# A planner's transfer model gets a fixed gap per transfer, and its searched order becomes a table

## The chip, the core and the metric

The kernel runs as one program on one core of a Trainium2 chip. Five engines work side by side, each with its own queue of instructions that it takes in order: PE (TensorE, matmuls and transposes; its weight loads are listed apart as PEld), DVE (VectorE), ACT (ScalarE), POOL (GpSimd) and SP (SyncE, which here only issues DMA transfers). The time is that of one execution on the device in microseconds (us); lower is better.

## The reference

Attention with rotary embedding for 4 batches of 8 heads, 576 positions, head size 64, then two matmul blocks on 2304 tokens:

```python
q_rot, k_rot = rotate(q), rotate(k)
scores = scale * q_rot @ k_rot.T              # 576 x 576 per head, softmax over rows
x = softmax(scores) @ v                       # -> 2304 x 512
h1 = ((x @ w1) * (x @ w2)) @ w3 @ w_out       # 512 -> 1024 -> 1024 -> 512
h2 = max(h1 @ u1, h1 @ u2, h1 @ u3)           # 512 -> 768
out = h2 @ u_out                              # 768 -> 512
```

The weights of the two matmul blocks arrive as 8-byte floats and are turned into 4-byte ones on the chip.

## The kernel before

**Stages.** For each of 16 pairs of heads the kernel loads q and k (`prepare`), rotates them, splits each into a high and a low part (matmuls run as three products of such parts), computes scores on PE into a two-buffer PSUM ring, takes the row maximum on DVE (L668), the exponential on ACT (L671), transposes the probabilities on PE (L676), copies them out of PSUM as a high part (L441, on ACT or DVE) and a low part (L708, DVE), and multiplies by v (`pv`). Beside this, in the first 200 us, weights are converted (`convert`): a 512 KB load into `raw` (two buffers), an ACT pass (L506), a DVE shift (L509) and a DVE merge (L511). From the converted w3 and w_out, `fold` makes the product w3 @ w_out: 8 blocks of 4 PE tasks (tile `m`), each block copied to `ga` and written to memory (`wp_d`). `gates` multiplies attention's output by w1 and w2 (tile `m` too). After attention come the rest of the fold (`fold_rest`), the product with it (`y_unit`), the second block by a Strassen-like scheme (`u_group`, tiles `q`, `tmp`, `top`) and the last matmul.

**What sets the order.** No engine's order is written out by hand. Every piece of work is a task with an engine, a modelled duration, dependences and a priority; there are 4349 tasks, numbered in the order in which the code adds them, and 1024 of them may go on either of two engines (`k.opts`, the first one is the default). `Plan.order` is a list scheduler: it keeps a clock per engine and always emits, on the engine that is free first, the ready task of lowest priority number. The emitted order is the program order of each engine, and dependences become semaphore waits. Before the change, the priorities came from formulas in the code, moved by some 400 random moves replayed from stored seeds (`MOVES`, `move`, `draws`), which also picked the engines.

**The model of a transfer.** A load or store is an SP task of 0.5 us with a `tail`, its size in units of about 350 KB (a 512 KB `raw` load has 1.46, a 256 KB store 0.73, a 576 KB q or k load 1.64, a 160 KB store 0.5). In `order`, one clock `dma` stands for all transfers: a transfer starts when the one before is through, and not before 0.65 us after the issue; it occupies 0.95 times its tail (1.9 times before 5 us), and lands 0.3 times its tail plus 0.9 us after that.

Of the kernel before, what the change touches and what calls it, by code (L numbers as in the profile page):

```python
# [45 lines left out]
MOVES = (  # L46
# [50 lines left out]
def draws(seed):  # L97
    mask = (1 << 64) - 1
    s = (seed * 0xD1342543DE82EF95 + 1) & mask
    while True:  # L100
        s = (s + 0x9E3779B97F4A7C15) & mask
        z = ((s ^ (s >> 30)) * 0xBF58476D1CE4E5B9) & mask
        z = ((z ^ (z >> 27)) * 0x94D049BB133111EB) & mask
        yield z ^ (z >> 31)


def move(prio, pick, opts, place, seed):


    d = draws(seed)  # L110

    def uni():
        return (next(d) >> 11) * (1.0 / 9007199254740992.0)

    def stretch(parts):
        width = len(prio) / parts
        lo = uni() * (len(prio) + width) - width
        return lo, lo + width

    kind = next(d) >> 62  # L120
    if kind == 1:
        parts, share = (32, 128, 512, 2048)[next(d) >> 62], (0.03, 0.1, 0.3, 1.0)[next(d) >> 62]
        lo, hi = stretch(parts)
        for i in range(len(prio)):
            if opts[i] > 1 and lo <= place[i] < hi and uni() < share:
                pick[i] = int(uni() * opts[i])
        return
    if kind == 0:
        by, width = (0.3, 1.0, 3.0, 10.0)[next(d) >> 62], 1 << (next(d) >> 61)
        lo = int(uni() * (len(prio) + width)) - width  # L130
        x = uni() + uni() + uni() + uni() - 2.0
        for i in range(max(lo, 0), min(lo + width, len(prio))):
            prio[i] = prio[i] + by * 1.7 * x
        return
    by, share = (0.1, 0.3, 0.6, 1.5)[next(d) >> 62], (0.01, 0.03, 0.1, 0.3)[next(d) >> 62]
    parts = (1, 8, 32, 128)[next(d) >> 62]
    lo, hi = stretch(parts)
    if parts == 1:
        share *= 0.3
    for i in range(len(prio)):  # L140
        if lo <= place[i] < hi and uni() < share:
            x = uni() + uni() + uni() + uni() - 2.0
            prio[i] = prio[i] + by * 1.7 * x
# [1067 lines left out]
```

## Time and profile before

| | |
|---|---|
| median of 3 runs | 925.85 us (925.26 to 926.72) |
| profiled execution, its own time | 927.38 us |
| its span, first to last instruction | 925.4 us |
| PE busy in the span | 891.0 us (96%) |
| DVE busy | 633.0 us (68%) |
| ACT busy | 475.9 us (51%) |
| POOL busy | 342.4 us (37%) |
| DMA queue of SP | 109.29 MB, 37.4% of 16 engines' span |

The profiled execution took 1.53 us more than the median, and 1.98 us of its time lie outside the span. Busy times of PE include the time in which matmuls overlap in its pipeline. The granted clock of TensorE is given as a share of full speed (2.4 GHz); its other level is 1.2 GHz.

### The profile page before, as it was taken

Reading aid. Unit: us, or ns where it says so; the run is one execution under the profiler, and the core shown is the slowest. Engines: PE = TensorE matmul, PEld = TensorE weight load, DVE = VectorE, ACT = ScalarE, POOL = GpSimd, SP = SyncE. Lnnn points to the kernel's source line nnn. Section 1 sums busy time; section 2 is a strip of 40 time slices with the busy share of each in tenths; the row PEclk is TensorE's granted clock in tenths of the full one; section 3 lists DMA queues with packets and bytes.
Section 4 is the critical chain, followed back from the end, with each engine's and each line's share of the span. In section 5 each row is a group of like instructions: output and inputs, shape, how many; then the busy total and the mean of one; then the engine's idle time right before and its main releaser. Section 6 shows DMA issues by size and latency. Waiting matters only on the chain.

```text
span 925.4 us, 16273 instructions
## 1 busy us (share of the span) xinstructions
PE 891.0 (96%) x5922; PEld 823.8 (89%) x5922; DVE 633.0 (68%) x1133; ACT 475.9 (51%) x1054; POOL 342.4 (37%) x332
## 2 busy tenths in 40 slices
PE   1898999999999999999999999999999999999998
PEld 1666769989999999999998999999999999999886
DVE  6997988898867677687766333657988577578300
ACT  4677887876757577567544222434323322334411
POOL 3645767766436366522110000433332333232000
PEclk9999999999999999999999999999999999999999
DMA  8454546542333123310147543323324114255511
GB/s 265 134 188 153 165 154 209 149 142 84 100 103 97 44 92 93 97 50 18 37 153 213 199 127 89 103 86 97 98 86 140 55 46 148 68 163 195 201 57 68
DMA packets 80287, 110.31 MB, mean 119 GB/s; under 512 B 27984, under 2 KB 61008, under 8 KB 80208
## 3 DMA queue, kind: packets, MB, share of 16 engines
q1 hardware_dynamic: 80208, 109.29, 37.4%
q8 instruction: 46, 0.75, 0.3%
q14 instruction: 33, 0.27, 0.1%
HBM read 83.76 MB, written 25.50 MB: 118 GB/s over the span
## 4 chain that ended last, share of the span: by engine, by line
PE 80%; DVE 9%; DMA 7%; issue 2%; ACT 1%; SPq 1%; POOL 0%; DVEq 0%; ACTq 0%
PE q L423 46%; PE m L423 15%; PE t L676 7%; PE pv L423 6%; PE s L423 6%; DVE pt L708 3%; DMA raw<-in_w3t_dram 3%; DVE sm L668 2%; DMA raw<-in_w_dram 2%; DVE raw L509 1%; DMA rawc<-in_w3t_dram 1%; SPq L444 1%; DMA vr<-in_vv_dram 1%; DVE cw L511 1%; ACT pt L441 0%
## 5 line engine op out<-in xcount | busy, mean ns | idle before, releaser
L708 DVE TENSOR_TENSOR pt<-t,pt 128x320 fp32r<-128x320 f32 (+3 forms) x256 | 132.4, 528 | 34.5 <-ACT pt L441 29.4
L441 ACT CAST pt<-t 128x320 fp32r<-128x320 f32 (+3 forms) x234 | 103.5, 456 | 51.9 <-PE t L676 24.9
L423 PE MATMUL pv<-pt,v 128*128 128x256 f32 (+1 forms) x576 | 113.2, 317 | 5.1 <-DVE pt L708 4.0
L668 DVE TENSOR_REDUCE sm<-s 128x1 f32<-128x576 f32 x144 | 103.9, 749 | 19.8 <-PE s L423 18.8
L423 PE MATMUL q<-gt,wp 128*128 128x384 f32 x576 | 100.0, 334 | 0.0
L423 PEld LDWEIGHTS q<-gt,wp 128*128 128x128 f32 x576 | 99.8, 188 | 0.0
L423 PEld LDWEIGHTS pv<-pt,v 128*128 128x128 f32 x576 | 82.8, 189 | 15.7 <-DVE pt L708 9.5
L423 PE MATMUL s<-st 64*128 64x288 f32 x768 | 71.7, 316 | 18.7 <-ACT st L618 11.7
L423 PEld LDWEIGHTS s<-st 64*128 64x128 f32 x768 | 55.6, 190 | 32.5 <-ACT st L618 11.7
L423 PE MATMUL q<-yc__7620,u 128*128 128x384 f32 x378 | 71.2, 340 | 0.0
L423 PE MATMUL q<-yc__7946,u 128*128 128x384 f32 x378 | 70.8, 340 | 0.0
L423 PE MATMUL q<-yc__7376,u 128*128 128x384 f32 x378 | 70.5, 340 | 0.0
L423 PEld LDWEIGHTS q<-yc__7946,u 128*128 128x128 f32 x378 | 67.1, 188 | 0.1
L423 PEld LDWEIGHTS q<-yc__7620,u 128*128 128x128 f32 x378 | 67.1, 188 | 0.0
L423 PEld LDWEIGHTS q<-yc__7376,u 128*128 128x128 f32 x378 | 67.1, 188 | 0.0
L441 ACT COPY tmp<-q 128x384 f32<-128x384 f32 x45 | 21.5, 479 | 84.7 <-PE q L423 84.5
L441 ACT COPY ga<-q 128x512 f32<-128x512 f32 (+2 forms) x34 | 16.9, 497 | 65.6 <-PE q L423 61.6
L1066 POOL TENSOR_TENSOR tmp<-tmp 128x384 f32<-128x384 f32 x20 | 22.6, 1132 | 72.3 <-ACT tmp L441 72.3
L423 PE MATMUL q<-tail,tail 128*128 128x512 f32 x216 | 49.1, 389 | 0.0
L423 PEld LDWEIGHTS q<-tail,tail 128*128 128x128 f32 x216 | 40.5, 188 | 8.4
L522 DVE TENSOR_TENSOR gt<-gt 128x768 fp32r<-128x768 f32 x24 | 26.7, 1117 | 25.3 <-ACT gt L521 25.3
L1079 DVE TENSOR_TENSOR tmp<-q,tmp 128x384 f32<-128x384 f32 x54 | 29.9, 554 | 15.4 <-PE q L423 15.2
(1222 smaller groups left out, 2050.9 us busy)
## 6 DMA issues: line engine op xcount, KB each, us to landing
gt<-g_d SPq DMA_DIRECT2D x24, 384.0 KB
raw<-in_m_dram SPq DMA_DIRECT2D x72, 128.0 KB
raw<-in_w_dram SPq DMA_DIRECT2D x16, 512.0 KB
h_d<-top SPq DMA_DIRECT2D x36, 192.0 KB
tail<-h_d SPq DMA_DIRECT2D x36, 192.0 KB
raw<-in_wo_dram SPq DMA_DIRECT2D x12, 512.0 KB
raw<-in_w3t_dram SPq DMA_DIRECT2D x12, 512.0 KB
g_d<-ga SPq DMA_DIRECT2D x32, 160.0 KB
```

The source lines that it names most:

```text
L423: pe.matmul(o, a, b, start=start, stop=stop, **kw)
L441: (e.copy if e is act else e.tensor_copy)(o, i)
L444: return add("SP", .5, lambda: sync.dma_start(o(), src()), r, w, part, deps, prio, tail=us)
L509: add("DVE", 0.42, lambda: dve.tensor_scalar(low_word(), low_word(), 29, None, ALU.logical_shift_right), part=[raw], deps=raw.writers, pri ...
L511: add("DVE", 0.69, lambda: dve.scalar_tensor_tensor(u(), u(), 3, low_word(), ALU.logical_shift_left, ALU.bitwise_or), r=[raw], deps=[first ...
L522: either(sb(n, "DVE"), lambda on: on.tensor_tensor(sel()[:, LO], f32(sel()[:, LO]), f32(sel()[:, HI]), ALU.subtract), r=[dst], part=[dst], ...
L668: add("DVE", c_dve(S), lambda s=s, col=col: dve.tensor_reduce(sm.t[:, 0, col:col + 1], s.t[:, :, :288], axis=AX.XY, op=ALU.max, negate=Tru ...
L676: pe.transpose(o, x, ident.t)
L708: add("DVE", c_dve(n), lambda: dve.tensor_tensor(low(pt.t), src(t.t), f32(hi(pt.t)), ALU.subtract), r=[t], part=[pt], deps=[h], prio=prio)
L1066: either(sb(TN), lambda on: on.tensor_tensor(s5.t, s1.t, s5.t, ALU.add), r=[s1], w=[s5], prio=prio)
L1079: add("DVE", c_dve(TN), lambda: dve.tensor_tensor(e.t, at_(o), e.t, ALU.add), r=[accs[o]], w=[e], prio=prio)
```

## The change

A transfer that starts after 12 us now occupies the DMA clock for 0.4 us more than its bytes, and lands 0.7 us after that, whatever its size. The formulas' priorities and the stored moves are no longer used: the rank of each task stands in a table `PLACE` (a permutation of 0 to 4348, entry n for task n), and `OTHER` lists the 168 tasks that go on their second engine. What the kernel computes, its tasks, their dependences, tiles and buffers stay as they are.

```diff
-MOVES = (
-    10000024, 10000032, 10000048, 10000067, 10000110, 10000112, 10000169, 10000173, 10000183, 10000227, 10000237,
...
+PLACE = (
+    2, 0, 1, 6, 3, 7, 21, 23, 25, 27, 29, 4, 5, 10, 14, 19, 20, 22, 28, 32, 35, 38, 18, 8, 12, 9, 11, 24, 26, 36, 45,
...
-def draws(seed):
...
-def move(prio, pick, opts, place, seed):
...
+OTHER = (
+    20, 21, 48, 57, 64, 143, 149, 152, 153, 184, 273, 282, 284, 344, 364, 411, 413, 414, 415, 523, 524, 529, 552,
...
             if k.tail:
                 dma = max(dma, end + 0.65)
-                dma += (1.9 if dma < 5.0 else 0.95) * k.tail
-                end = dma + 0.3 * k.tail + 0.9
+                if dma < 12.0:
+                    dma += (1.9 if dma < 5.0 else 0.95) * k.tail
+                    end = dma + 0.3 * k.tail + 0.9
+                else:
+                    dma += 0.4 + 0.95 * k.tail
+                    end = dma + 0.7
...
-        prio = [k.prio for k in self.tasks]
-        place = {k.num: i for i, k in enumerate(self.order(prio)[1])}
-        pick = [0] * len(prio)
-        for seed in MOVES:
-            move(prio, pick, [len(k.opts) for k in self.tasks], place, seed)
+        other = set(OTHER)
         for k in self.tasks:
-            k.eng, k.dur, k.lock = k.opts[pick[k.num]]
-        best = self.order(prio)
+            k.eng, k.dur, k.lock = k.opts[k.num in other]
+        best = self.order(PLACE)
```

**The tables read against the order before.** Sorted by `PLACE`, a task stands on average 6 places of 4349 from where it was emitted before, at most 94. The first 24 tasks on PE, the first 10 on ACT and the first 4 on SP are the same. The moves in the first 100 us that the next sections speak of, by number of the task on its engine:

| task | engine | number before | number in the table |
|---|---|---|---|
| second exponential of pair 0 (33) / v of pair 1 (158) | ACT | 11 / 10 | 10 / 11 |
| shift L509 and merge L511 of the first w_out chunk (2107, 2108) | DVE | 22, 38 | 14, 17 |
| load of the third w_out chunk (2113) | SP | 28 | 21 |
| its shift and merge (2115, 2116) | DVE | 51, 56 | 24, 40 |
| the four PE tasks of `fold(0)` (2125 to 2128) | PE | 46, 48, 50, 53 | 30, 34, 39, 45 |
| load of w3 chunk f=5 (2171), the one issued at 67.22 us | SP | 48 | 40 |
| load of w3 chunk f=3 (2151) | SP | 42 | 37 |

The engine differs for 83 tasks: 37 go from ACT to DVE, 28 from POOL to DVE, 12 from DVE to POOL, 4 from DVE to ACT, and one each way between ACT and POOL. By their starts in the trace before, none lies ahead of 28 us; 7 lie between 50 and 200 us (6 of them onto DVE, one from POOL to ACT); 13 between 350 and 400 us, all onto DVE; 26 between 650 and 725 us (19 onto DVE, 7 from it).

## Rows read from the trace of the kernel before

**Rows 1.** Busy time by stage: start:end, length, each engine's busy us (instructions), clock, DMA.
```profile
0.00:28.00 28.00, 8.94 (x45) 7.29 (x47) 18.21 (x23) 13.19 (x26) 12.14 (x13) 1.00 0.72 224
28.00:150.00 122.00, 111.75 (x733) 83.09 (x732) 107.11 (x197) 97.55 (x233) 74.38 (x62) 0.99 0.53 166
150.00:475.00 325.00, 323.63 (x2640) 304.00 (x2639) 247.92 (x477) 216.24 (x539) 158.66 (x145) 1.00 0.29 89
475.00:925.00 450.00, 446.72 (x2512) 429.44 (x2510) 259.75 (x439) 148.91 (x260) 97.18 (x114) 1.00 0.38 122
```
**Rows 2.** PE's waits from 28 to 150 us: sum us, times, longest.
```profile
PE pv L423 <- DVE pt L708: 3.8, 6, 1.5
PE t L676 <- DVE pt L708: 1.4, 4, 0.9
PE t L676 <- DVE sm L683: 1.2, 2, 0.9
...
PE s L423 <- ACT p__474 L671: 1.2, 1, 1.2
```
**Rows 3.** DVE's waits on transfers, 25 to 150 us.
```profile
DVE raw L509 <- DMA raw<-in_w3t_dram: 3.2, 3, 1.4
DVE raw L509 <- DMA raw<-in_w_dram: 2.1, 2, 1.2
```
**Rows 4.** Timeline of PE, 36 to 80 us: start, us, instruction [idle before].
```profile
46.24 1.06 PE L423 MATMUL s<-st,z__109 128*128 128x288 f32 x6 [1.22 <-ACT p__474 L671]
...
67.32 0.28 PE L676 MATMUL t<-ident,sm 128*9 128x128 f32 x1 [0.92 <-DVE sm L683]
...
76.10 0.41 PE L423 MATMUL pv<-pt,v 128*128 128x320 f32 x1 [1.54 <-DVE pt L708]
77.42 0.33 PE L676 MATMUL t<-ident,p__528 128*128 128x128 f32 x1 [0.90 <-DVE pt L708]
```
**Rows 5.** The chain of waits between 60 and 80 us: start, us, what.
```profile
67.22 6.05 DMA raw<-in_w3t_dram
...
73.29 1.58 DVE raw L509
```
**Rows 6.** Timeline of SP: issues from 58 to 68 us.
```profile
59.76 0.99 SPq L444 DMA_DIRECT2D raw<-in_w3t_dram  x2
60.80 0.42 SPq L444 DMA_DIRECT2D wp_d<-ga  x1
63.17 0.33 SPq L444 DMA_DIRECT2D qk__688<-in_qk_dram  x1
...
66.50 0.33 SPq L444 DMA_DIRECT2D wp_d<-ga  x1
```
**Rows 7.** Timeline of ACT: the exponential at 19.39, two loads issued in a row.
```profile
18.75 0.72 ACT L638 CAST v<-vr 128x640 fp32r<-128x640 f32 x1 [0.20 <-DMA vr<-in_vv_dram]
19.39 0.73 ACT L671 ACTIVATE p__187<-s,sm 128x576 f32<-128x576 f32 x1
...
73.28 0.68 ACT L506 ACTIVATE w<-raw 128x512 f32<-128x512 f32 x1 [1.90 <-DMA raw<-in_w3t_dram]
...
74.48 0.68 ACT L506 ACTIVATE w<-raw 128x512 f32<-128x512 f32 x1 [0.21 <-DMA raw<-in_w3t_dram]
```
**Rows 8.** Timeline of DVE, 13 to 35 us.
```profile
21.88 0.76 DVE L668 TENSOR_REDUCE sm<-s 128x1 f32<-128x576 f32 x1 [1.54 <-PE s L423]
...
26.73 1.64 DVE L509 TENSOR_SCALAR raw<-raw 128x512 uint32<-128x512 uint32 x1
28.29 0.68 DVE L708 TENSOR_TENSOR pt<-t,pt 128x512 fp32r<-128x512 f32 x1
...
32.16 0.69 DVE L441 CAST pt<-t 128x512 fp32r<-128x512 f32 x1
```
**Rows 9.** Busy time by stage, as in rows 1, around DVE's fullest stretches.
```profile
50.00:200.00 150.00, 143.55 (x1005) 114.99 (x1005) 129.90 (x231) 120.60 (x287) 100.36 (x84) 1.00 0.55 171
...
640.00:800.00 160.00, 160.00 (x909) 160.00 (x908) 121.21 (x229) 48.29 (x93) 53.80 (x77) 1.00 0.28 89
```

More of the change, by code (lines that the diff above doesn't have):

```diff
@@ L42 @@
 TERMS = ((HI, HI), (LO, HI), (HI, LO))
-MOVES = (
[47 rows of a table removed]
-)
-def draws(seed):
[L98 to L104, printed above, removed]
-def move(prio, pick, opts, place, seed):
[L110 to L143, printed above, removed]
+PLACE = (
[221 rows of a table added]
+)
+OTHER = (
[9 rows of a table added]
+)
 class Task:
```

274 rows, old and new, of tables (MOVES, OTHER, PLACE) are left out of this document.

## Prediction

> **What bounds the kernel now.** I read four views, from coarse to fine. First the busy time by stage [rows 1], columns PE, PEld, DVE, ACT, POOL: from 150 us on PE is never out of work for long. It is idle for 325 - 323.63 = 1.4 us up to 475 us, and for 3.3 us after that, which is its last matmul's end, the copy out and the last store. So three quarters of the run are PE-bound, and no order of tasks shortens them, since the change takes no matmul away. What an order can win lies ahead of 150 us: 28 - 8.9 = 19 us of idle PE before 28 us and 122 - 111.75 = 10.25 us between 28 and 150 us. There DVE is busy for 107.1 of 122 us, 88%, the most loaded engine beside PE.
>
> Second, who PE waits for between 28 and 150 us [rows 2]: the low part of the probabilities on DVE (3.8 + 1.4 us), the softmax sums on DVE (1.2), the exponentials on ACT (1.2 for one of them), which wait in turn for DVE's maxima. PE waits for no transfer itself. Third, what DVE waits for [rows 3]: 3.2 + 2.1 = 5.3 us in front of L509, the first DVE step of a weight conversion, for a load of 512 KB that has not landed. DVE takes its queue in order, so everything behind L509 stands too, the softmax among it. Fourth, the chain of waits from 60 to 80 us shows one such case whole [rows 5]: a load issued at 67.22 lands at 73.27, L509 runs until 74.87, and PE meanwhile has its two idle stretches of 1.54 and 0.90 us [rows 4].
>
> **The transfer model against the trace.** This load is the one that the old formula misses. From the issues ahead of it [rows 6] (a second q/k load like that of 63.17 follows it), by hand: the pair at 59.76 starts at 59.76 + 0.5 + 0.65 = 60.91; old occupancies are 1.39 for a raw load, 0.69 for a wp_d store, 1.56 for a q or k load. The queue is through with the first five transfers at 67.5, with the store of 66.50 at 68.3, with our load at 69.8, and that one lands 1.34 later, at 71.1. With 0.4 more for each and 0.7 at the end the same sum gives 73.1. The row says 73.27: the new form is right here by 0.2 us, the old one 2.2 us early, and a plan made with the old one puts L509 where DVE must stand still. But the gap is no property of each transfer: the raw load issued right behind this one lands 74.48 - 73.28 = 1.20 us after it [rows 7], where the old form spaces the two by 1.39 and the new by 1.79. So the new model is right in a mixed queue and too slow for neighbours of one kind; a plan made with it keeps more room than needed, which costs only where the early work is in the way.
>
> A rule of the Trainium skill speaks against the change (DMA: Bandwidth & Descriptors, section Anatomy of one DMA): it puts the fixed part of a transfer's time, about 2 us, in the completion, not in setting up, so that it would delay the landing and not the transfer behind. The pair of rows 7 agrees with it, the late load of rows 5 does not; by the rule alone the new charge would order transfers no better than the old one, and the sum below would be that of the third rival.
>
> **The change part by part.** The new formula itself runs nowhere on the chip; what changes is the order and 83 engines. I read `PLACE` as the order itself, though the planner may still swap tasks that aren't ready.
>
> *Start.* ACT does the second exponential of pair 0 before v of pair 1 rather than after it. That copy held ACT from 18.75 to 19.39 [rows 7], and PE's next scores wait for this exponential. It may now start 0.64 us earlier. Behind it the chain goes on over DVE, which then waited 1.54 us for PE [rows 8], so DVE can follow. The two steps 2107 and 2108 (1.64 us at 26.73, 0.7 later) move ahead of that idle time and use it up in part. I take -0.5 us, bounds 0 and -0.65.
>
> *fold(0) earlier.* Its four PE tasks move 16 to 8 places ahead, into the stretch with the wait of 1.22 us at 46.2 [rows 4]. For that the third w_out load is issued 7 places earlier and the first raw buffer is freed earlier by 2108. What goes early on DVE (2115, 2116) takes the place of 2107 and 2108, one pair for the other, so DVE's load between 26 and 40 us stays. I take -1.2 us, the whole wait, since a ready matmul stands there; bounds 0 and -1.2.
>
> *Loads of w3 earlier.* Load 2171 goes from place 48 to 40, past two q/k loads, four v loads and a store; its buffer is freed by chunk f=3, whose load goes from 42 to 37 and whose DVE steps go up too. The three idle stretches of PE at 67.3, 76.1 and 77.4 sum to 0.92 + 1.54 + 0.90 = 3.36 us [rows 4]. All three follow on an L509 that waited. If the data is there, L509 still costs its own time on DVE, so I take -2.5, bounds 0 and -3.4. The v and q/k loads that it passes are for later pairs and have many us in hand.
>
> *Engines.* Between 50 and 200 us six tasks move onto DVE, copies out of PSUM like that of 0.69 us at 32.16 [rows 8], which is the largest shape: at most 4.1 us on an engine that has 150 - 129.9 = 20.1 us free there [rows 9]. Covered mostly; where it falls in front of a probability, PE waits. I take +0.3, bounds 0 and +4.1 if every one does. From 640 to 800 us a net 21 tasks move onto DVE, again none over about 0.7 us, hence at most 15 us against 160 - 121.2 = 38.8 us of free DVE [rows 9]; ACT and POOL give work away that didn't bind. Cost 0, hidden by those idle times while PE stays full; without that cover it would be part of the 15 us.
>
> *The rest of the gaps.* Of 10.25 us, 10.25 - 1.22 - 3.36 = 5.7 remain, most of them DVE behind with softmax work. A search may close some; I take 0, bounds 0 and -5.7.
>
> Sum: -0.5 - 1.2 - 2.5 + 0.3 = -3.9 us. Against the profiled execution that is 927.38 - 3.9 = 923.5; the median lies 1.53 us lower, so 925.85 - 3.9 = 921.95, say 922.0 us.
>
> **The rivals.** *Given back later.* DVE paces the stretch up to 150 us. If PE's gain up to 80 us only makes it arrive earlier at work that DVE hasn't done, what counts is what DVE saves: 3.2 us of waits for w3 loads [rows 3], less four tasks added before 150 us at up to 0.69 = 2.8 us. That leaves about 0.4, with the 0.5 of the start 0.9: 925.0 us. For it: 88% busy on DVE. Against: DVE has 15 us free, and each fold that comes early is one less later.
>
> *More than I count.* The search also closes most of the other 5.7 us; then -3.9 - 5 = -8.9: 917.0 us. For it: they are waits of the same kind. Against: they aren't waits for transfers, and the tasks' durations in the model didn't change (L509 took 1.64 us in one place where the model has 0.42).
>
> *No gap, no effect.* If transfers land as the pair of rows 7 does, loads were late by chance of one queue, and the new order is as good as the old: 925.9 us.
>
> *Slower: L509 waits earlier.* 2115 now stands at number 24 on DVE, right before the first low probabilities, which ran at 28.29 [rows 8]. Its load can't be issued before 2108 has freed the buffer, about 20 us. A raw load took up to 6.05 us [rows 5] and lands at 26.1 then: just in time. If it lands after 28.3 us, DVE stands with the whole softmax behind it, and PE with nothing else. Each us later costs one; issued at 24, behind v loads, it would cost about 2. To end above 927.7 the early conversions, five of them before 60 us, must each wait 1.2 us as the worst of rows 3 did, 6 us in all, against the 3.9 gained: 928.0 us.
>
> **How the numbers follow.** The forecast, between 919.5 and 924.0, has 0.47; more than I count (below 919.5) 0.15; given back and no effect together 0.28 (0.20 and 0.08); slower 0.10. The likeliest is 922.0 us. Runs of this kernel lie within 0.16% of each other, so 0.2% (1.85 us: below 924.0, above 927.7) is about what can be told from no change. Faster is 0.47 + 0.15 = 0.62, same 0.28, slower 0.10. For 8 in 10 the range leaves out the far third of the good case (below 916.5) and the slower one with the top of the same: 916.5 to 926.5.
>
> **What would show it.** In the profile after: PE's idle time from 28 to 150 us down from 10.25 to about 6.5; no stretch of 1.5 us near 75 us and none of 1.2 near 46; DVE's waits for raw loads down from 5.3 to under 3 us; the first fold matmuls at 42 to 48 us instead of 54; the second exponential at about 18.7; PE without idle time from 150 us on, also from 640 to 800 us. Given back: those gaps closed, but new ones of the same sum between 80 and 150 us. Slower: an L509 that waits between 20 and 40 us. Wrong for another reason: the planner's order differs from the table's ranks, or PE waits for DVE after 640 us.

## The result and the profile after

The change makes the kernel slower: 934.24 us median of 4 runs (931.77 to 935.85) against 925.84 us for the kernel before on the same chip, a ratio of 1.0088 with a 95% interval of 1.0064 to 1.0112. The forecast was 922.0, with a tenth of the chance on slower. The profiled execution took 935.85 us, its span is 934.0 against 925.4. Lines of this kernel.py stand 139 lower than before: L509 is L648 here, L511 L650, L423 L562, L708 L847.

Busy time by stage, in the columns of [rows 1] (the last stage runs to the end of the trace):

```profile
0.00:28.00 28.00, 9.76 (x52) 7.74 (x53) 20.13 (x27) 14.51 (x28) 12.29 (x13) 1.00 0.81 254
28.00:150.00 122.00, 110.16 (x693) 80.52 (x694) 108.23 (x192) 92.41 (x219) 72.91 (x59) 0.96 0.49 153
150.00:475.00 325.00, 320.68 (x2605) 299.09 (x2604) 250.88 (x488) 209.45 (x519) 155.24 (x141) 1.00 0.29 91
475.00:945.00 470.00, 454.85 (x2577) 436.97 (x2575) 270.87 (x478) 147.12 (x257) 95.08 (x104) 1.00 0.37 117
```

PE is idle for 11.84 us from 28 to 150 us, where before had 10.25 and I expected 6.5, and for 4.3 us from 150 to 475 us, where it was never out of work for long (1.4). Its busy time sums to 895.4 us against 891.0, with the same matmuls: of the 8.6 us that the span grew, 4.4 are matmuls that took longer and 4.2 are idle. The waits of PE from 28 to 150 us (compare [rows 2]), and DVE's wait for a raw load from 25 to 150 us (compare [rows 3]):

```profile
PE pv L562 <- DVE pt L847: 4.3, 6, 1.8
PE t L815 <- DVE pt L847: 1.9, 3, 0.8
PE m L562 <- DVE w L650: 1.7, 1, 1.7
```
```profile
DVE raw L648 <- DMA raw<-in_w3t_dram: 0.8, 1, 0.8
```

So what the change models did come: DVE waits 0.8 us for loads instead of 5.3. But there is a new wait, PE at the matmuls of fold(0) for a merged weight. Two timelines of that place, DVE and GpSimd (start, us, instruction):

```profile
44.91 0.88 DVE L648 TENSOR_SCALAR raw<-raw 128x512 uint32<-128x512 uint32 x1
45.71 3.05 DVE L650 SCALAR_TENSOR_TENSOR w<-w,raw 128x512 uint32<-128x512 uint32 x2
48.79 1.51 DVE L847 TENSOR_TENSOR pt<-t,pt 64x320 fp32r<-64x320 f32 x3
```
```profile
44.10 1.40 POOL L751 TENSOR_TENSOR qk__421<-qk__421,tabs__122 128x576 f32<-128x576 f32 x1
45.47 1.61 POOL L751 TENSOR_TENSOR qk__421<-qk__421,tabs__128 128x576 f32<-128x576 f32 x1
47.03 1.18 POOL L910 TENSOR_TENSOR x__318<-x__318,rb 128x256 f32<-128x256 f32 x1
```

The shift ends at 45.79, 0.29 us after GpSimd's product that began before it (44.10 + 1.40 = 45.50); the second merge ends at 48.76, 0.55 after the product that ends at 48.21. Three steps of weight conversions (one shift, two merges) that take 0.42 + 2 x 0.68 = 1.8 us elsewhere hold DVE for 3.9, and the low parts of the probabilities stand behind them. PE's timeline, and the stages around it, column PEclk after the five engines:

```profile
45.05 0.42 PE L562 MATMUL pv<-pt,v 128*128 128x320 f32 x1 [1.80 <-DVE pt L847]
48.81 2.08 PE L562 MATMUL m<-wo,w 128*128 128x512 f32 x2 [1.65 <-DVE w L650]
```
```profile
42.00:46.00 4.00, 2.20 (x17) 1.87 (x15) 4.00 (x7) 3.10 (x7) 3.92 (x4) 1.00 0.46 170
46.00:50.00 4.00, 2.35 (x10) 1.36 (x8) 3.92 (x5) 0.95 (x3) 2.21 (x2) 0.55 0.32 85
50.00:54.00 4.00, 4.00 (x16) 2.70 (x14) 2.60 (x5) 0.91 (x3) 0.00 (x0) 0.59 0.48 177
```

After the first of the two waits the granted clock falls to its lower level, 1.2 GHz, and fold(0) runs there: by an estimate from the two lines PE loses another 2.35 x 0.45 + 4.00 x 0.41 = 2.7 us of full-speed work. The trace of before has one such stretch as well (0.72 in 36 to 42 us, as here), but nothing in 42 to 60 us.

**Where the time goes, by PE's progress.** For each trace I took the moment at which PE had done the first W us of its matmul tasks (each task weighed with its median duration over all traces) and subtracted that of the kernel before; plus means later. This is worked out from the traces, not a view of the profile; each line is one execution, and the runs are told below.

```
W done, us (moment in before)   15    35    60    80   120   150   190   290   410   500   880
                              (32)  (52)  (73)  (92) (123) (148) (177) (250) (337) (402) (704)
after                         -1.1  +3.6  +5.4  +2.7  +2.5  +4.0  +5.3  +5.5  +8.3 +10.1  +8.7
e1  new to 60 us, then old    -1.1  +4.3  +5.1  +3.2  +3.7  +4.1  +4.7  +4.4  +4.3  +4.3  +4.1
e4  old, new engines          -0.7  -0.6  -0.1  -1.8  -1.7  -0.5  -0.3  -0.8   0.0  +0.3  +0.3
e7  old, fold chain moved     +0.2  +4.4  +6.2  +4.6  +4.5  +4.6  +4.8  +4.4  +4.4  +4.4  +5.2
e8  old, w3 loads early       +0.5  +0.5  +2.4  -0.2  -0.1  -0.1  -0.1  -0.6  -0.6  -0.6  -0.9
e9  new, two products out     -0.6  +0.1  +2.1  -0.5  -0.7  +1.7  +2.9  +3.3  +4.0  +5.9  +4.5
e10 old, two products out     -0.4  -0.6  -0.5  -2.4  -1.8  -1.7  -0.9  -1.4  -1.4  -1.4  -1.5
e11 old, w_out half moved     +0.8  +2.2  +2.7  +0.8  +1.0  +1.1  +1.0  +1.4  +1.4  +1.3  +1.0
e12 new to 40 us, then old    -1.1  +0.4  +1.5  -0.4  +0.2  -0.2  +0.4  +0.1  +0.1  +0.1  -0.1
e13 new, 34 products out      +0.2  +0.5  +2.6  -0.6  -0.9  +0.6  +0.5  +0.8  +1.5  +3.3  +1.9
e14 old, 34 products out      -0.1  +1.3  +1.2  -0.8  -1.0  -1.8  -2.0  -3.5  -3.5  -3.5  -3.4
e15 new, GpSimd exchanged     -1.0  -0.3  +2.7  +0.1  +1.1  +2.9  +4.2  +4.8  +5.5  +7.3  +5.9
e16 the same to 100, then old -0.6  +0.1  +2.2  -0.5  +1.6  +1.8  +1.9  +1.6  +1.6  +1.6  +1.7
e17 old to 90, then new       -0.2  -0.1  +0.3  -1.6  -2.0  +0.4  +0.9  +1.2  +1.8  +3.7  +2.1
e18 old to 150, then new      -0.2  +1.8  +1.3  +0.2  +0.1   0.0  +1.7  +2.3  +3.3  +5.1  +4.7
```

Two losses: 4 to 5 us at 40 to 55 us, and 4 to 6 more, net, behind 120 us (in the changed kernel +2.5 to +10.1 by 402 us, of which 1.4 come back).

How far one execution can be trusted is in the table too (35 runs of before on one chip took 923.87 to 930.67 us, 0.7%, where the prediction had 0.16% from three). Four replays have the old order between 73 and 92 us of before (e4, e10, e11, e12). At 92 us they stand between -2.4 and +0.8, so a difference of 2 us up to there says little by itself; behind 250 us three of them (e10, e11, e12) run level with before to 0.4 us. And all four gain 1.7 to 1.9 us on before between 60 and 80 us of work: of the 2.7 us that the changed kernel gains there, most is that the one trace of before was late at this place, and not the new order.

### The profile page after: what moved, and what is told of

Its sections match the earlier page's. It is cut to its first block, busy times and chain, and to the rows that moved or that the text cites. A ratio compares the mean times of both kernels' runs of the same rounds, so it can differ in the third digit from the quotient of the medians.

```text
span 934.0 us, 16262 instructions
## 1 busy us (share of the span) xinstructions
PE 895.4 (96%) x5922; PEld 824.3 (88%) x5922; DVE 650.1 (70%) x1182; ACT 463.5 (50%) x1021; POOL 335.5 (36%) x316
## 4 chain that ended last, share of the span: by engine, by line
PE 85%; DVE 6%; DMA 3%; ACT 3%; issue 2%; POOL 1%; SPq 0%; ACTq 0%; DVEq 0%; POOLq 0%
PE q L562 47%; PE m L562 17%; PE t L815 8%; PE pv L562 7%; PE s L562 6%; DVE pt L847 2%; DVE sm L807 1%; DMA raw<-in_w3t_dram 1%; DVE raw L648 1%; DMA raw<-in_wo_dram 1%; ACT pt L580 1%; DMA qk__3076<-in_qk_dram 1%; DMA qk__116<-in_qk_dram 1%; DVE w L650 0%; POOL qk__3086 L751 0%
## 5 line engine op out<-in xcount | busy, mean ns | idle before, releaser
L847 DVE TENSOR_TENSOR pt<-t,pt 128x320 fp32r<-128x320 f32 (+3 forms) x256 | 132.9, 528 | 37.1 <-ACT pt L580 32.7
L580 ACT CAST pt<-t 128x320 fp32r<-128x320 f32 (+3 forms) x222 | 99.2, 457 | 60.8 <-PE t L815 28.3
L562 PE MATMUL pv<-pt,v 128*128 128x256 f32 (+1 forms) x576 | 116.7, 320 | 7.7 <-DVE pt L847 5.7
L562 PEld LDWEIGHTS pv<-pt,v 128*128 128x128 f32 x576 | 83.7, 190 | 19.2 <-DVE pt L847 9.2
L562 PE MATMUL q<-gt,wp 128*128 128x384 f32 x576 | 100.0, 334 | 0.0
L562 PEld LDWEIGHTS q<-gt,wp 128*128 128x128 f32 x576 | 99.8, 188 | 0.0
L562 PE MATMUL s<-st 64*128 64x288 f32 x768 | 72.3, 316 | 17.1 <-ACT st L757 12.1
L562 PEld LDWEIGHTS s<-st 64*128 64x128 f32 x768 | 55.7, 190 | 31.7 <-ACT st L757 12.1
L562 PE MATMUL q<-yc__7618,u 128*128 128x384 f32 x378 | 71.5, 339 | 0.0
L562 PE MATMUL q<-yc__7937,u 128*128 128x384 f32 x378 | 71.0, 339 | 0.0
L562 PE MATMUL q<-yc__7376,u 128*128 128x384 f32 x378 | 70.2, 339 | 0.3 <-DVE tmp L1218 0.3
L562 PEld LDWEIGHTS q<-yc__7937,u 128*128 128x128 f32 x378 | 66.8, 188 | 0.4 <-DVE tmp L1218 0.3
L562 PEld LDWEIGHTS q<-yc__7376,u 128*128 128x128 f32 x378 | 66.4, 188 | 0.7 <-DVE tmp L1218 0.6
L562 PEld LDWEIGHTS q<-yc__7618,u 128*128 128x128 f32 x378 | 66.9, 188 | 0.0
L580 ACT COPY tmp<-q 128x384 f32<-128x384 f32 x39 | 18.7, 479 | 84.0 <-PE q L562 83.9
L562 PE MATMUL q<-tail,tail 128*128 128x512 f32 x216 | 49.1, 389 | 0.0
L562 PEld LDWEIGHTS q<-tail,tail 128*128 128x128 f32 x216 | 40.6, 188 | 8.4
```

What stands on the lines that cost most here:

```text
L562: pe.matmul(o, a, b, start=start, stop=stop, **kw)
L580: (e.copy if e is act else e.tensor_copy)(o, i)
L847: add("DVE", c_dve(n), lambda: dve.tensor_tensor(low(pt.t), src(t.t), f32(hi(pt.t)), ALU.subtract), r=[t], part=[pt], deps=[h], prio=prio)
```

## The experiments

Before and after are compared in pieces. So each experiment writes the order out as one list, and the planner replays it instead of choosing (it still computes times, to give buffers their slots); the engines come from `OTHER`:

```diff
-        best = self.order(PLACE)
+        best = self.order(EMIT)
...
-        while len(done) < len(tasks):
...
+        for n in emit:
+            k = tasks[n]
+            e = k.eng
+            at = max(clock[e], ready[n])
```

Times are medians, each against the kernel before on the same chip.

**Order or engines (e3, e4).**

```diff
 e3: EMIT = the order after
-    OTHER = the engines after
+    OTHER = the engines before
 e4: EMIT = the order before
-    OTHER = the engines before
+    OTHER = the engines after
```

> The whole new order, but every task on the engine it had before (83 tasks back, 65 of them off DVE). If the engines lose (DVE gets 49 tasks more): 925 to 928. If the order loses: 932 to 936, as the changed kernel.

> The order of the kernel before, written out, with the 83 new engines. If the engines lose: 930 to 935. If the order loses and the engines cost nothing: 925 to 927. A task that changes its engine without its neighbours being moved could also stall on the new engine's queue: then it is slower by more than the changed kernel, and says nothing against the engines in the new order.

e3: 933.96, ratio 1.0064 (1.0046 to 1.0082). e4: 927.23, ratio 1.0004 (0.9989 to 1.0018). The 83 engines cost nothing that can be told in the whole; the order loses. e4 also shows that replaying adds nothing that can be measured.

**Early or late (e1, e2, e17, e18, e12).**

```diff
 EMIT =
+    e1: 244 tasks of the order after, then the order before
+    e2: 267 tasks of the order before, then the order after
+    e17: 428 of the order before, then after; e18: 821 of it, then after
+    e12: 151 of the order after, then before
```

> The order is written out as one list and replayed: the first 244 tasks (about the first 60 us) in the changed kernel's order and engines, all that follow in the order and engines of the kernel before. If the early stretch loses (fold(0)'s matmuls and the w_out merges moved up, a lag of about 4 us at 60 us in the trace after): 928.5 to 931. If the loss comes behind 60 us (the rest of the order, or the 83 engines, of which few lie before 60 us): 924 to 926.

> The other splice: the first 267 tasks in the order and engines of the kernel before, all that follow as in the changed kernel. If the early stretch alone loses: 925 to 927. If the lag of another 4 to 5 us, which the trace after shows growing between 150 and 300 us, is a loss of the later order by itself: 929 to 931. If all of the loss lies behind 60 us: 933 to 936.

> The first 428 tasks (90 us) in the order and engines of the kernel before, all that follow as in the changed kernel; the splice lies behind the w3 chunks, where the first splice at 60 us had stood still for 7 us. If the later order loses by itself, whatever came before it: 4 to 6 above before, 930.5 to 933, with the steps of the lag at 125 to 150, 180 and 370 us. If it loses only behind its own late start: within 1.5 of before.

> The same with the splice at 150 us (821 tasks). If a third of the later loss lies between 100 and 150 us (the step of about 2 there) and the rest behind: 2 to 3.5 above before. If it all lies before 150 us: within 1 of before.

> The first 151 tasks (40 us) in the changed kernel's order, the rest as before. The new order was 1.1 us ahead at 15 to 40 us in its trace. If that is a gain of the order that survives: 924.5 to 925.5 where before is 926.5. If the start differs from execution to execution by as much (replays of the old start lay between 1.2 ahead and 0.5 behind): the same as before within 0.7.

e1: 933.27, 1.0055 (1.0037 to 1.0072): the early stretch alone loses, and by the table nothing more is lost behind it. e2: 939.33, 1.0127 (1.0107 to 1.0146), more than the changed kernel: at the seam, where one order takes over from the other, DVE waits 8.0 us for two w3 loads whose buffers the two orders free differently, so its sum says nothing. e17 was cut behind the w3 chunks: 929.77, 1.0028 (1.0015 to 1.0041), under the range that I gave. Its progress shows why: this execution was 2.0 us ahead at 120 us and 2.1 behind at the end, a loss of 4.1. e18: 930.83, 1.0038 (1.0020 to 1.0056); it loses from 150 us on, so the loss does not end there. So the later order loses by itself. e12: 925.80, 0.9990 (0.9975 to 1.0004): the first 40 us of the new order are no measurable gain, and no version here that computes the whole beats the kernel before.

**Which part of the early order (e7, e11, e6, e5).** The chain of fold(0) is its w_out and first two w3 conversions with their loads (tasks 2106 to 2124 and 2131 to 2134) and its four matmul tasks (2125 to 2128).

```diff
 e7: EMIT = the order before
+    2106 to 2128 and 2131 to 2134 at their places after
 e11: EMIT = the order before
+    2106 to 2120 at their places after
 e6: EMIT = the order after
+    2125 to 2128 at their places before (their copy 2129 and store 2130 behind them)
 e5: EMIT = the order after
+    2106 to 2128 and 2131 to 2134 at their places before
+    (2129, 2130, 2141 to 2143 and 2152 to 2154 shift behind them)
```

> The kernel before, replayed, with that one chain of 31 tasks at the changed kernel's places and nothing else moved. If the chain makes the early loss: 929 to 932, 3 to 6 above before. If the loss needs the rest of the new order: within 1 us of before.

> The kernel before, replayed, with only the w_out part of the chain at the changed kernel's places (15 tasks: loads, casts, shifts and merges of the four w_out chunks); w3 and fold(0) stay. If the loss of the whole chain (4.8 by the run that moved it alone) comes from the w3 merges and fold(0): within 1 of before. If the w_out merges among the first softmaxes make it: 928.5 to 931.

> The changed kernel with the four matmul tasks of fold(0) alone back at their old places on PE; every cast, shift and merge stays early. If the loss is PE standing at fold(0) for a weight merge that is not done (1.65 us at 47.16 in the trace after) and the clock that falls behind it: 929 to 932. If the loss is the merges on DVE, which ran 1.92 and 1.21 us in place of 0.69 beside GpSimd and held up the softmax: no gain, 933 to 936.

> The changed kernel, replayed, with the whole chain of fold(0) back where the kernel before had it: the loads, casts, shifts and merges of the w_out chunks and of the first two w3 chunks (27 tasks), and the four matmul tasks. The loads behind it that use the same two raw buffers shift with it. If this chain makes the early loss of 4 to 6 us: 2 to 6 below the changed kernel, 928.5 to 932 on a chip where before is 926 to 927. If the early loss comes from the other moved tasks of the first 60 us: 933 to 936.

(The chain has 27 tasks with its matmuls; the first and last of these expectations count them as 31.) e7: 931.26, 1.0048 (1.0031 to 1.0066): this one chain, moved in the old order, makes the early loss. e11: 926.91, 1.0003 (0.9991 to 1.0016): its w_out half costs nothing, so it is the w3 half and the matmuls. e6: 933.14, 1.0068 (1.0051 to 1.0085): with the matmuls back PE doesn't wait for the weight, but for the low parts, 5.2 us in all from 37 to 60 us, and within the intervals as much is lost. The matmuls were not the cause. e5: 945.45, 1.0198 (1.0179 to 1.0217), a miss: the two raw buffers, shared with the later w3 chunks that stayed early, make DVE wait 8.9 us for loads between 50 and 75 us; moving the chain back alone is no test.

**GpSimd beside the merges (e9, e10, e15, e16).** e9 and e10 leave out two products and so compute something else.

```diff
 e9 (order after), e10 (order before):
         for k in best[1]:
+            if k.num in (409, 410):
+                continue
             k.emit()
 e15 (order after), the same on GpSimd in e16:
-    403, 404, 405, 409, 410, 134
+    403, 404, 405, 134, 409, 410
 e16: its first 475 tasks, then the order and engines before
```

> The changed kernel, replayed, with two of GpSimd's products left out (the two table multiplications of one k tile, 409 and 410, 44.10 to 47.08 us in the trace after; the tile stays unrotated). They run beside the w3 merges, which took 1.92 and 1.21 us on DVE there. If GpSimd beside them stretches the merges and the softmax behind them is late by that: the merges take 0.68 each, PE's waits of 1.80 and 1.65 us near 45 us shrink, and the time falls by 2 to 5, to 929 to 932. If the place in DVE's queue alone makes the loss: within 1 of the changed kernel, 933 to 935.

> The control: the kernel before, replayed, with the same two products left out (45.59 and 48.24 us there). No merge of w3 ran beside them, so under either theory it is within 1 of before; what it gains is to be taken off what the other run with the products left out gains.

> The changed kernel, replayed, with one exchange on GpSimd and nothing left out: the product by rb (134), which has to wait for a load that lands at 46.24 us, stands ahead of the two table products 409 and 410, so that GpSimd is idle from 44 to 46 us, where the w3 merges run. If GpSimd beside the merges makes the early loss: 929 to 931.5, 3 to 5 below the changed kernel. If not: 933 to 935, or more, since the products come 3 us later.

> The same exchange, and the order and engines of the kernel before from the 476th task on (about 100 us). If the early loss is GpSimd beside the merges and the rest is the order behind 100 us: both are gone, 925 to 927, as before, and no better than before by over 1. If the early stretch loses in another way too: 928 to 930.

e9: 930.20, 1.0027 (1.0014 to 1.0040). e10: 926.29, 0.9992 (0.9980 to 1.0005). The products cost the new order about 5 us more than the old one (0.0088 - 0.0027 less 0.0008, of 926; 2 to 8 us by the intervals). e15, which computes everything: 930.67, 1.0035 (1.0019 to 1.0052). Its lines, DVE (shift L621, merge L623), GpSimd, and the stages:

```profile
45.14 0.42 DVE L621 TENSOR_SCALAR raw<-raw 128x512 uint32<-128x512 uint32 x1
45.47 1.29 DVE L623 SCALAR_TENSOR_TENSOR w<-w,raw 128x512 uint32<-128x512 uint32 x2
```
```profile
46.72 0.73 POOL L883 TENSOR_TENSOR x__318<-x__318,rb 128x256 f32<-128x256 f32 x1 [2.08 <-DMA rb<-r_d]
47.41 1.41 POOL L724 TENSOR_TENSOR qk__421<-qk__421,tabs__122 128x576 f32<-128x576 f32 x1
```
```profile
42.00:46.00 4.00, 3.49 (x23) 2.91 (x20) 3.00 (x6) 2.86 (x7) 2.56 (x2) 0.69 0.47 182
46.00:50.00 4.00, 4.00 (x23) 2.61 (x22) 3.68 (x8) 2.03 (x5) 3.28 (x3) 1.00 0.71 225
50.00:54.00 4.00, 4.00 (x32) 3.08 (x32) 3.27 (x7) 3.56 (x8) 0.92 (x2) 1.00 0.09 38
```

GpSimd is idle for 2.08 us, the three conversion steps are done at 46.76 instead of 48.76, PE is full from 46 to 54 us at full clock. The early loss is gone in the table (-0.3 at 52 us against +3.6), although the clock stood at its lower level here too, a little earlier (0.69 in 42 to 46 us). So it is shown that GpSimd's products beside these steps make most of the early loss; up to some 2 us may be left (at 92 us e15 stands at +0.1, the four replays of the old order between -2.4 and +0.8). e16: 929.20, 1.0030 (1.0018 to 1.0042), more than the 925 to 927 that I expected if the two causes were all. It is the other outcome, 928 to 930: the new order loses in another way too, ahead of its end at 100 us or at the seam. By the table it loses 2.1 us between 80 and 120 us of work, around its seam at 100 us, where e15 loses 1.0, and nothing behind.

**Is the later loss the same (e13, e14)?** Both leave out 34 products on GpSimd (36 to 200 us), and so part of the computation.

```diff
         for k in best[1]:
+            if k.num in (403, 404, 405, 409, 410, 534, ..., 1066):
+                continue
             k.emit()
```

> The changed kernel, replayed, with 34 of GpSimd's products left out: all multiplications and additions by the tables that run on GpSimd between 36 and 200 us (51 of GpSimd's 111 us there; the tiles stay unrotated). If GpSimd beside DVE explains the later loss too (1.72 us for a shift of 0.42 ahead of PE's wait of 1.20 at 166.54 us): within 2 of the control with the same products left out. If the later order is tighter by itself: 4 to 5 above that control.

> The control: the kernel before with the same 34 products left out. If GpSimd beside DVE costs the old order little: 924 to 927. If it costs both orders alike: it falls with the other, to 920 to 923, and the distance between the two stays near 8.

e13: 927.84, 1.0008 (0.9998 to 1.0018). e14: 923.23, 0.9955 (0.9937 to 0.9973). Without the products the old order gains 3.5 us too, so what they cost is no loss of the new one alone (whether it is GpSimd beside DVE, or that the products were waited for, these two runs do not separate). 4.6 us stay between the two, about the later half, and by the table they all arise late: at 123 us the two stand level (-0.9 and -1.0). With the products out the new order still loses 1.5 us from 123 to 148 us and 1.8 from 337 to 402 us, as the changed kernel does, but not the 1.3 from 148 to 177 us. Single waits there are of that kind: in the changed kernel a shift of 1.72 us, beside a GpSimd product that ends 0.28 us before it, stands before PE's wait of 1.20 us for a low part (DVE, GpSimd, PE),

```profile
164.24 1.72 DVE L648 TENSOR_SCALAR raw<-raw 128x512 uint32<-128x512 uint32 x1
165.88 1.41 DVE L807 TENSOR_REDUCE sm<-s 128x1 f32<-128x576 f32 x2
167.22 0.47 DVE L847 TENSOR_TENSOR pt<-t,pt 128x320 fp32r<-128x320 f32 x1
```
```profile
164.25 1.43 POOL L753 TENSOR_TENSOR qk__1791<-qk__1791 128x576 f32<-128x576 f32 x1
```
```profile
167.74 0.71 PE L562 MATMUL pv<-pt,v 128*128 128x320 f32 x3 [1.20 <-DVE pt L847]
```

and in e13 that idle stretch is gone. Others remain, in e17 for instance:

```profile
PE s L535 <- ACT p__1536 L783: 1.1, 1, 1.1
PE t L788 <- DVE pt L820: 0.8, 1, 0.8
```

These are PE's two longest waits from 120 to 145 us. In the changed kernel's trace DVE takes the two maxima ahead of that exponential nine and thirteen places behind the maximum before them, where the old order takes them one right after the other. That this order of the maxima makes the wait was not tried. And from 360 to 420 us PE looks busy in both orders, but does less in the new one (e18, then e16 with the old order there):

```profile
360.00:420.00 60.00, 59.41 (x483) 54.94 (x482) 45.77 (x91) 34.38 (x85) 22.46 (x23) 1.00 0.21 64
```
```profile
360.00:420.00 60.00, 59.89 (x492) 56.74 (x491) 42.21 (x82) 38.54 (x97) 26.85 (x26) 1.00 0.21 66
```

483 matmuls against 492 at full clock. By the table 0.4 to 1.6 us of what is lost up to 402 us come back by 704 us, and e4, with the old order and the new engines, loses 1.1 us between 250 and 402 us, so a part of it is the engines. Which neighbours on PE make the rest was not tried; this part stays open.

**The third term by itself (e8).**

```diff
 EMIT = the order before
+    ACT: 2132 behind 2122; 2152 behind 202
+    DVE: 2134 behind 176; 2153 behind 201; 2154 behind 185
+    SP: 2151 behind 2121; 2171 behind 419
```

> The kernel before, replayed, with seven tasks moved: the cast and merge of the second w3 chunk from 53.57 and 57.94 us to about 50 us, so that its raw buffer is free earlier, the load, cast, shift and merge of the fourth chunk behind it from 59.76 to about 52 us, and the load of the sixth (issued 67.22 us before) to about 60 us. This is the predicted third term by itself. If the late landing at 73.27 us sets PE's gaps there: they go and the time falls by 1.5 to 2.5, 923.5 to 924.5 where before is 926. If DVE's own queue sets them: within 0.5 of before.

e8: 927.80, 1.0011 (0.9999 to 1.0023). No gain, where 1.5 to 2.5 was expected if the late landing sets the gaps. The stretches of 1.54 and 0.90 us near 75 us [rows 4] are gone but for 0.42, but the first of them was largely that one execution's: in e4, with the old order here, the load lands 4.83 us after its issue, not 6.05 as in [rows 5], and PE's gaps at the same two matmuls are 0.38 and 0.90.

```profile
67.12 4.83 DMA raw<-in_w3t_dram
```
```profile
74.84 0.42 PE L535 MATMUL pv<-pt,v 128*128 128x320 f32 x1 [0.38 <-DVE pt L820]
76.15 0.33 PE L788 MATMUL t<-ident,p__528 128*128 128x128 f32 x1 [0.90 <-DVE pt L820]
```

By the table e8 gains 2.6 us on the kernel before between 60 and 80 us of work, 0.7 to 0.9 more than the replays of the old order do. And it had lost 1.9 just ahead (they 0.1 to 1.1), with two new waits:

```profile
56.02 1.10 PE L528 MATMUL m<-wo,w 128*128 128x512 f32 x2 [1.54 <-DVE w L616]
60.44 0.86 PE L528 MATMUL pv<-pt,v 128*128 128x256 f32 x5 [1.04 <-DVE pt L813]
```

So DVE's queue looks like the bound here, as the rival "given back later" had it: a conversion done earlier is paid for in the softmax that it goes ahead of. The traces are one execution each, and sizes of 1 us are at the edge of what they show; the median shows that nothing is won.

## Why the prediction was wrong

**The transfer model: right in kind, and for the one load by luck so near.** The prediction's sum, done with the issue times of the same load in six replays with the old order there (e4, e10, e12, e14, e17, e18; an estimate), gives a landing between 0.4 us too early and 1.1 too late with the new charge, and 0.6 to 1.7 too early with the old one. The new form is nearer in five of the six; that it met the one trace to 0.2 us was luck. DVE's waits for raw loads fell to 0.8 us (under 3 was forecast; 4.0 to 5.3 in the replays of the old order e4, e10, e11 and e12, 1.5 to 2.5 in those of the new one e3, e9 and e15), and the idle stretch of PE near 75 us to 0.75. The rule of the Trainium skill that the prediction sets against the change (DMA: Bandwidth & Descriptors, section Anatomy of one DMA) stands there for transfers that GpSimd issues, while SyncE issues all of these; no run here separates a gap from a late completion. What the charge of 0.4 us does apart from the order that the search found was not tried.

**Start, -0.5: not to be told from 0.** The second exponential of pair 0 starts at 17.28 us (18.7 forecast), but replays of the old start lay between 1.2 us ahead and 0.5 behind the one trace that I had, and e12 is within 0.25% of before.

**fold(0) earlier, -1.2: the step that failed; it is about +4.** Two sentences of it don't hold. "DVE's load between 26 and 40 us stays" holds there, but with the loads two w3 chunks also went up, to 44 to 49 us, beside GpSimd's products, where three conversion steps took 3.9 us for 1.8. "A ready matmul stands there": it was not ready, PE stood 1.65 us before it, and the clock fell behind the waits. The sign was in my rows: an L509 of 1.64 us [rows 8]. I carried it as the step's own time and did not ask what ran beside it. Moved alone, the chain of fold(0) costs 1.0048, 4.4 us (e7).

The Trainium skill has the rule (SBUF — State Buffer, section Who interferes with whom): a DVE instruction that needs the port pair shared with GpSimd and a GpSimd instruction exclude each other for the whole instruction, and the later one waits. The traces agree: all 28 shifts and merges over 0.75 us in the changed kernel, and all 30 in the kernel before, end 0.28 to 0.30 us (shift) or 0.54 to 0.55 us (merge) after the end of a GpSimd product. One of them, the shift of 164.24, waited through a product that began 0.01 us after it (164.25, shown with e13), so the recorded starts do not always say which of the two goes first. Since the trace of before shows the same stretching, the move could have been priced, as an estimate, at up to a product's 1.4 us for each shift or merge.

**Loads of w3, -2.5: mis-sized, about -0.9 in its place, and no gain in the end.** The changed kernel gains 2.7 us there (+5.4 to +2.7 between 60 and 80 us of work), but replays of the old order gain 1.7 to 1.9 of it as well: I had priced the gaps of one execution. The rival "no gap, no effect", loads late by chance, had more in it here than I allowed. The L509 of 1.58 us [rows 5], too, was not the step's own time: it ends at 74.87, 0.29 us after this product of the kernel before (73.16 + 1.42 = 74.58), so 1.2 us of it came from GpSimd and not from the load.

```profile
73.16 1.42 POOL L612 TENSOR_TENSOR qk__693<-qk__693,tabs__122 128x576 f32<-128x576 f32 x1
```

What is left is given back, by e8. The rival "given back later" named the reason, DVE paces this stretch; here it was given back ahead, not behind.

**Engines, +0.3: not contradicted** (e4, 1.0004, 0.9989 to 1.0018). From 640 to 800 us PE has no wait, as forecast; the 1.1 us that e4 loses between 250 and 402 us lie where I had no cost.

**From 150 us on, 0: wrong; with the stretch from 120 us it is 4 to 6.** "No order of tasks shortens them" is so, but an order can lengthen them; I had no term for that. The idle time rose from 1.4 to 4.3 us, and some matmuls came slower. One part, from 148 to 177 us, goes with GpSimd's products (e13); the cause of the rest stays open.

**The slower rival** had the right sign for another reason: no shift waited long for its load. The sign of another failure, an order that differs from the table's ranks, did not come: on their engines all but 70 of 4346 tasks stand where the table has them, and none of the 70 lies ahead of 150 us.

## What to carry to other kernels

Before an instruction is moved in an in-order queue, look at what runs on the neighbour engine at the new place: an instruction that took four times its usual time once has a reason there, and at its new place it may meet the same reason. Before a gap is priced, see whether other executions of the same order have it: one of those that I priced was 1.54 us in one trace and 0.38 in a replay of the order there. A matmul put ahead as filler fills only if its own inputs have slack; else it is a new wait at the head of the queue. To split a change of order, replay both orders as lists and cut where no shared buffer is between two owners: two of the splices here stood still at their seam and told nothing.

## What the runs showed of the hardware

Shift and merge take 0.42 and 0.68 us with no GpSimd instruction beside them (at most 0.43 and 0.69 in the changed kernel) and up to 1.72 and 1.92 with one. That the long ones all end a fixed time after a GpSimd product says that the recorded duration contains the wait: a busy DVE is in part a waiting one.

TensorE's clock stood at its lower level for a part of 36 to 42 us in some executions and not in others, with the same 38 matmuls there: 0.72 in the changed kernel, 1.00 in e9. It cost little: PE was busy for 5.63 us in the one and for 3.94 in the other, where it waited instead. The fall at 46 us cost time because fold(0) ran in it.
